# Moving the first loads to a second queue, and the fills and filler products around them, in a three-stage attention and MLP kernel

## The chip, the cores and the metric

The kernel runs on one NeuronCore of a Trainium2 chip. The metric is the time of one execution in microseconds on the device, given as the median of several runs. The core has five engines that run side by side, each through its own queue of instructions in a fixed order: PE (matrix products), DVE (vector), ACT (scalar and activation functions), POOL (general purpose) and SP, which only issues transfers between HBM and the on-chip memory. An instruction starts when it is at the head of its engine's queue and what it waits for has happened.

## What is computed

Linear attention mixed with causal attention, and behind it two MLPs with different activations. Cut to what matters:

```python
# q, k, v: (4, 8, 576, 64); M_prev: (4, 8, 64, 64); z_prev: (4, 8, 64); beta: (8,)
a     = softmax(causal(q @ k.T / 8));  local = a @ v
q_p   = elu(q) + 1
mem   = (q_p @ M_prev) / (q_p . z_prev + 1e-6)
g     = 1 / (1 + exp(-beta))
x     = g * mem + (1 - g) * local               # laid out as (2304, 512)
x     = softplus(x @ w_in) @ w_out              # 512 -> 2048 -> 512, weights given as float64
h     = x @ w2_in
P, Q  = a0 + a1 h + a2 h^2 + a3 h^3,  1 + |b0||h| + |b1|h^2
out   = (P / (Q + 1e-6)) @ w2_out
```

## The kernel before

All work is recorded first as operations with a key, and a planner (`Program.order`, L289) then lays every operation on its engine: it steps through an assumed timeline, takes on each engine the ready operation with the smallest key, and for operations that more than one engine can do (`flex`, L220) it also picks the engine. The result is a fixed order for each engine, which `emit` (L389) writes out; nearly all instructions therefore carry the line L392. A change at the start moves the assumed times behind it, and with them the order and the choice of engines of everything that follows, until the order falls into the same pattern again.

The attention runs in seven passes (`PASSES`, L63), each over one batch and some row tiles; a pass has two units of four heads (or four units of two). The first three passes work in float32: `attention32` (L1004) transposes q and k of a unit on PE (`transpose32`, L992, into banks of PSUM taken in turn from the list `B32`, L48), computes the scores of four heads on PE, masks them and takes their minimum on DVE (shown as CUSTOM_DVE_ANT_0), and exponentiates them on ACT. Between the passes run the blocks of the first MLP: `g1` (L1164) makes a pair of hidden tiles from the input weights, `g2` (L1207) multiplies them into the output. Before a float16 block, `xgroup` (L1084) splits its input x into a high and a low half per column chunk: four high halves on any of ACT, DVE and POOL (`scopy`, L533) and four low halves on DVE (one instruction) or POOL (two) (`low`, L553). `pmax` (L573) finds the scale that the split needs, by a reduction on POOL and a small product on PE.

The MLP weights come as float64, in pieces of 512 KB that SP loads as pairs of 32-bit words (`load_piece`, L1118) and DVE turns into float32 with three instructions a piece (`bits`, L1126: one TENSOR_SCALAR and two SCALAR_TENSOR_TENSOR on 128x512), or ACT and POOL share in it (`bits_abs`, L1132). There are 16 pieces of the input weights and 16 of the output weights, all in the first 100 us.

At the start, six raw buffers `RAW` (the landing places of q, k and v) have rows 64 to 127 filled with zeros by POOL (L1385), over all ten blocks of 64 columns; float32 units use only the first eight blocks, and fill them fully. `EARLY` (L29) says after which piece of the input weights the other first loads are issued: q and k of both first units after piece 0, v of unit 0 and the batch's M and z after piece 1, the three small constants (`beta` for the gate, and `a`, `b` of the second MLP) after piece 2. All are issued by SP. The gate's chain (`consts`, L603) is one Exp on ACT and six small instructions on DVE. PE is kept busy by 120 filler products of `mask` with itself (`WARM`, L1399), written into bank 0 and never read; the planner puts them wherever PE has nothing else.

Of the kernel before, what the change touches and what calls it, by code (L numbers as in the profile page):

```python
# [25 lines left out]

QLATE = 80
PORT = 0.8
EARLY = lambda load, u, consts, batch: (  # L29
    (lambda: load(u[0], 0, 1), lambda: load(u[1], 0, 1)),  # L30
    (lambda: load(u[0], 2), batch),
    (consts,),
    (lambda: load(u[1], 2),),
)
KEY_B0 = 30
KEY_S2 = 60
# [8 lines left out]
WR0 = 6  # L45
WARM = 120
FA32 = 3
B32 = (0, 1, 2, 3, 4, 5, 6)  # L48
PEC = 2.5
SIGN = ((0,), (0,))  # L50
SIGN2 = ((1,), (0, 0, 1))
# [5 lines left out]
SIGN3 = (0, 0, 1)  # L57
BACKLOG = 4000.0
NRAW = 6
NGH = 4  # L60
EXP = 0x7F800000

# [106 lines left out]
class Program:  # L169
# [14 lines left out]
    def add(self, eng, name, fn, kw, writes=()):  # L184
        rd, wr = [], list(writes)
        for k, v in kw.items():
            if is_ap(v):
                (wr if k in self.OUTS else rd).append(v)
        dma = 0
        if eng == "SP":  # L190
            o, i = kw["out"], kw["in_"]
            nb = width(o) * SIZE[o.dtype] * o.shape[0]
            if "transpose" in name:
                dur, dma = 1325, nb / 240.0

            else:
                run = min(SIZE[x.dtype] * (x.ap[-1][1] if x.ap[-1][0] == 1 else 1) for x in (o, i))
                dur, dma = 650 if o.shape[0] <= 64 else 475, nb / (360.0 if run >= 512 else 180.0)
        else:
            dur = cost(eng, name, kw)  # L200
        ported = shares_port(eng, name, kw)
        if self.cur is not None and self.cur.eng in (None, eng):
            op = self.cur
            op.eng = eng
            if eng in op.alts:
                op.alts[eng][0] += dur
                op.alts[eng][1].append((fn, kw))
            else:
                op.alts[eng] = [dur, [(fn, kw)]]
        else:  # L210
            op = self._new()
            op.eng = eng
            op.alts[eng] = [dur, [(fn, kw)]]
        op.dma = dma
        if ported:
            op.port.add(eng)
        self._deps(op, rd, wr)
        return op
# [70 lines left out]
    def order(self):  # L289
# [26 lines left out]
        while len(done) < len(self.ops):  # L316
# [52 lines left out]
            free[e] = end = s + dur  # L369
            for b in o.banks:  # L370
                held.setdefault(b, {})[e] = end
            if e == "SP":
                free["BULK"] = end
                dma_free = max(dma_free, s + min(dur, 650) + 625) + o.dma
                if dur > 1000:

                    free["SP"] = free["BULK"] = max(end, dma_free - 880)
                end = dma_free + 900
            done.append(o)
            for j in o.succ:  # L380
                q = self.ops[j]
                q.npred -= 1
                q.ready = max(q.ready, end + (max(LATENCY[e][x] for x in q.alts) if e in LATENCY else 0))
                if q.npred == 0:
                    release(q)
        self.span = max(free.values())
# [35 lines left out]
def attn_moe_moe2(ctx, tc, q, k, v, m_prev, z_prev, beta, w1i, w1o, w2i, w2o, ca, cb, out):  # L422
# [43 lines left out]
    def vw(o, shape, dtype):  # L466
        n = 1
        for s in shape:
            n *= s
        a = arena[:, o:o + n * SIZE[dtype] // 4]  # L470
        if dtype != F32:
            a = a.bitcast(dtype)
        if len(shape) == 1:
            return a
        names = [chr(97 + i) for i in range(len(shape))]
        return a.rearrange(f"p ({' '.join(names)}) -> p {' '.join(names)}", **dict(zip(names[1:], shape[1:])))
# [125 lines left out]

    def consts():  # L603
        P.bulk = True
        SP.dma_start(out=gg, in_=beta.partition_broadcast(128))
        SP.dma_start(out=aa, in_=ca.partition_broadcast(128))
        SP.dma_start(out=bb, in_=cb.partition_broadcast(128))
        P.bulk = False
        A.activation(out=gg, in_=gg, func=AF.Exp, scale=-1.0)
        ts(gg, gg, 1.0, None, ALU.add)  # L610
        V.reciprocal(gg, gg)
        ts(iog, gg, -1.0, 1.0, ALU.mult, ALU.add)
        ts(iog, iog, 2.0 ** -100, None, ALU.max)
        V.reciprocal(iog, iog)
        ts(iog15, iog, 2.0 ** -15, None, ALU.mult)
        A.activation(out=bb, in_=bb, func=AF.Abs)

    def consts2():
        A.activation(out=fa, in_=aa, func=AF.Abs)
# [79 lines left out]
        scopy(m.ms[:, :, 0, :], mr, m.s)  # L699
        stt(m.ms[:, :, 1, :], mr, m.s, m.ms[:, :, 0, :], ALU.mult, ALU.subtract)  # L700

    def load(u, *which):
        P.bulk = True
        load_(u, which)
        P.bulk = False

    def load_(u, which):
        p = u.p
        for i, (src, r, t0) in enumerate(((k, u.rk, 0), (q, u.rq, p.qts[0]), (v, u.rv, 0))):
            if which and i not in which:  # L710
                continue
            n = p.nk - t0
            r = r.rearrange("p (t h) d -> p h t d" if p.f32 else "p (h t) d -> p h t d", h=u.nh)
            if u.nh == 4:
                for t in range(n):
                    SP.dma_start(out=r[:, :, t, :], in_=src[p.b, u.h:u.h + 4, (t0 + t) * 128:(t0 + t + 1) * 128, :].rearrange("h p d -> p h d"))
            else:
                full = min(p.nk, 4) - t0
                for e in range(u.nh):
                    SP.dma_start(out=r[:, e, 0:full, :], in_=src[p.b, u.h + e, t0 * 128:(t0 + full) * 128, :].rearrange("(t p) d -> p t d", p=128))  # L720
                if p.nk == 5:
                    SP.dma_start(out=r[0:64, :, n - 1, :], in_=src[p.b, u.h:u.h + u.nh, 512:576, :].rearrange("h p d -> p h d"))
# [388 lines left out]
    def w_in_ap(w, pc):  # L1111
        p, i = divmod(pc, 2)
        return w.bitcast(U32)[i * 256:(i + 1) * 256, p * 512:(p + 1) * 512].rearrange("(c p) f -> p c f", p=128)

    def w_out_ap(w, pc):
        return w.bitcast(U32)[pc * 128:(pc + 1) * 128, :]

    def load_piece(ap, r):  # L1118
        P.bulk = True
        if len(ap.shape) == 3:  # L1120
            SP.dma_start(out=r.rearrange("p (c f) t -> p c (f t)", c=2), in_=ap)
        else:
            SP.dma_start(out=r.rearrange("p f t -> p (f t)"), in_=ap)
        P.bulk = False
# [194 lines left out]
    def w1_raw(which, pc):  # L1319
        if which == 0 and 0 <= pc - WR0 < 8:  # L1320

            return w1_o[pc - WR0].bitcast(U32).rearrange("p (f t) -> p f t", t=2)
        return vw(wraw[which][pc % len(wraw[which])], (512, 2), U32)

    def w1_load(which, pc):
        load_piece(w_in_ap(w1i, pc) if which == 0 else w_out_ap(w1o, pc), w1_raw(which, pc))

    def w1_place(which, pc, f32):
        if pc >= 16:
# [42 lines left out]
    def w2_early(i0, i1):  # L1372

        steps = [(0, pc) for pc in range(NST[0])] + [(1, pc) for pc in range(NST[1])]
        for i in range(i0, i1):
# [6 lines left out]
            w2_bits(which, pc, r, dst, a_t[1][:, 1024:1280].bitcast(BF16), vw(o, (512,), F32), SIGN3[i % len(SIGN3)])  # L1382
            SP.dma_start(out=w2d[which * 16 + pc], in_=dst)

    P.key = -180  # L1385
    for o in RAW:
        G.memset(vw(o, (10, D), F32)[64:128], 0.0)

    P.key = -150
    w1_load(0, 0)  # L1390
    P.add("POOL", "memset", lambda out: make_identity(nc, out), {"out": idf})
# [4 lines left out]

    P.pkey = 1e6
    for _ in range(WARM):
        PE.matmul(out=bank[0][:, 0:256], lhsT=mask[:, 0:128], rhs=mask[:, 0:256], start=True, stop=True)  # L1399
    early = EARLY(load, units, consts, lambda: batch_load(passes[0]))  # L1400
    for pc in range(16):
        P.key = -149 + pc
# [269 lines left out]
```

## Time and profile before

| | |
|---|---|
| median of three runs | 1015.4 us (1012.12, 1015.4, 1015.81) |
| the profiled execution, its own time | 1016.02 us |
| span of that execution's instructions | 1014.2 us |
| mean granted PE clock | 0.985 of full |
| busy share PE / DVE / ACT / POOL | 95% / 88% / 82% / 45% |

The span runs from the first instruction to the last; the execution's own time has 1.8 us around it. A busy PE is one with a product under way, filler products among them. Shares are means over stages with different limits, so the start, the middle and the end have to be read apart: a stage's limit is the engine that shows no idle time in it, while the others wait for it.

### The profile page before, as it was taken

The page shows a single profiled execution, that of the slowest core. Times are in us where ns is not written, and L with a number is a line of the kernel's source. Part 1 is how long each engine was busy: PE and PEld are TensorE (multiplying, and loading weights), DVE is VectorE, ACT ScalarE, POOL GpSimd, SP SyncE. Part 2 cuts the span into 40 slices and gives each one's busy share as a digit, 9 for nine tenths or more (in the row PEclk, how much of TensorE's full clock was granted, in tenths as well). Part 3 has the DMA queues.
Part 4 walks back from the last instruction along what each step waited for, and adds up shares of the span by engine and source line. Part 5 has one row for each costly group of instructions (what it writes and reads, how often), then busy time and mean ns, then how long its engine had stood idle before and what let it go on. Part 6 is the DMA issues. An engine that isn't in the chain of part 4 may idle for free. (4 is left out here: it accounts for less than half of the span.)

```text
span 1014.2 us, 22841 instructions
## 1 busy us (share of the span) xinstructions
PE 959.6 (95%) x8256; PEld 696.0 (69%) x8256; DVE 893.1 (88%) x2193; ACT 826.8 (82%) x1934; POOL 455.6 (45%) x516
## 2 busy tenths in 40 slices
PE   7779999999979999999899999899999999999998
PEld 6547688788769888888888998445555555555553
DVE  6999778988899988899878999988989889798886
ACT  4886988888869999899887888867888787887875
POOL 3121566873342243342325343655655455555443
PEclk9969999999989999999999999989999999999999
DMA  9997347568689979998998664000001000000000
GB/s 249 317 227 200 66 102 145 123 121 158 130 170 168 153 144 163 184 182 193 209 282 267 219 207 144 1 1 32 32 1 63 1 32 32 1 32 2 32 1 31
DMA packets 249889, 122.08 MB, mean 120 GB/s; under 512 B 219184, under 2 KB 225328, under 8 KB 249776
## 3 DMA queue, kind: packets, MB, share of 16 engines
q1 hardware_dynamic: 249776, 120.63, 51.4%
q8 instruction: 64, 1.05, 0.4%
q14 instruction: 49, 0.40, 0.1%
HBM read 65.54 MB, written 15.73 MB: 80 GB/s over the span
## 5 line engine op out<-in xcount | busy, mean ns | idle before, releaser
L392 PE MATMUL bank<-arena,w 128*128 128x160 f16 (+3 forms) x4288 | 414.8, 256 | 12.0 <-DVE arena L392 7.3
L392 PE MATMUL bank<-arena 128*128 128x384 f16 (+10 forms) x2852 | 355.6, 299 | 24.3 <-DVE arena L392 8.6
L392 PEld LDWEIGHTS <-w 128*128 128x128 f16 x3840 | 292.8, 98 | 29.9 <-issue 18.7
L392 ACT ACTIVATE arena<-bank,tiny 128x384 f32<-128x384 f32 (+8 forms) x504 | 276.3, 587 | 41.4 <-PE bank L392 34.6
L392 PEld LDWEIGHTS <-arena 128*128 128x128 f16 (+1 forms) x2464 | 165.8, 105 | 119.8 <-issue 29.8
L392 POOL TENSOR_TENSOR arena<-arena 128x384 f32<-128x384 f32 (+8 forms) x165 | 167.9, 1021 | 166.3 <-ACT arena L392 104.1
L392 PE MATMUL bank<-arena,gr 128*128 128x512 f16 x864 | 202.8, 380 | 1.2 <-POOL gr L392 1.1
L392 PEld LDWEIGHTS <-gr 128*128 128x128 f16 x864 | 84.5, 98 | 95.5 <-POOL gr L392 2.5
L392 POOL TENSOR_TENSOR gr<-arena,gr 128x384 f16<-128x384 f32 x96 | 90.6, 944 | 103.6 <-issue 81.2
L392 POOL TENSOR_SCALAR arena<-arena,tiny 128x512 f16<-128x512 f32 (+9 forms) x94 | 71.6, 768 | 102.2 <-DVE tiny L392 31.9
L392 ACT ACTIVATE bank<-bank,tiny 128x320 f32<-128x320 f32 (+5 forms) x192 | 103.3, 545 | 14.5 <-DVE tiny L392 9.5
L392 ACT ACTIVATE bank<-bank 128x320 f32<-128x320 f32 (+2 forms) x208 | 104.8, 504 | 1.6
L392 ACT ACTIVATE arena<-bank 128x320 f16<-128x320 f32 (+5 forms) x147 | 72.2, 501 | 29.6 <-PE bank L392 16.6
L392 PEld LDWEIGHTS bank<-arena,w 128*128 128x128 f32 x448 | 83.1, 190 | 12.4 <-issue 1.5
L392 DVE SCALAR_TENSOR_TENSOR arena<-arena,tiny 128x512 f16<-128x512 f32 (+5 forms) x101 | 89.8, 903 | 1.8 <-POOL arena L392 1.1
L392 DVE SCALAR_TENSOR_TENSOR bank<-bank,tiny,lt 128x384 f32<-128x384 f32 x96 | 59.6, 621 | 34.0 <-ACT lt L392 32.3
L392 ACT ACTIVATE lt<-arena,qe 128x384 f32<-128x384 f32 x96 | 59.0, 614 | 32.6 <-POOL arena L392 31.0
L392 DVE SCALAR_TENSOR_TENSOR arena<-arena,qe,lt 128x384 f32<-128x384 f32 x96 | 76.0, 791 | 0.7 <-ACT lt L392 0.7
L392 DVE SCALAR_TENSOR_TENSOR arena<-bank,tiny,arena 128x384 f16<-128x384 f32 (+4 forms) x112 | 64.0, 591 | 8.9 <-ACT arena L392 8.4
L392 DVE TENSOR_SCALAR tiny<-tiny 128x1 f32<-128x1 f32 (+8 forms) x349 | 64.5, 208 | 6.4 <-ACT bank L392 5.1
L392 DVE CUSTOM_DVE_ANT_0 bank<-bank,mask,tiny 128x384 f32<-128x384 f32 (+4 forms) x112 | 66.8, 605 | 2.4 <-PE bank L392 2.0
L392 PEld LDWEIGHTS bank<-arena 128*128 128x128 f32 (+3 forms) x412 | 43.2, 168 | 29.2 <-ACT arena L392 8.1
(122 smaller groups left out, 1143.3 us busy)
## 6 DMA issues: line engine op xcount, KB each, us to landing
arena<-in_moe_w_out_dram SPq DMA_DIRECT2D x32, 512.0 KB, 5.0
arena<-in_moe_w_in_dram SPq DMA_DIRECT2D x24, 512.0 KB, 5.1
w2d<-a SPq DMA_DIRECT2D x24, 256.0 KB, 3.0
arena<-w2d SPq DMA_DIRECT2D x24, 256.0 KB, 4.6
arena<-in_k_dram SPq DMA_DIRECT2D x44, 128.0 KB, 3.1
arena<-in_v_dram SPq DMA_DIRECT2D x44, 128.0 KB, 2.9
arena<-arena SPq DMA_DIRECT2D x32, 160.0 KB, 2.9
arena<-x2d SPq DMA_DIRECT2D x6, 768.0 KB, 4.3
```

The lines of the kernel that those rows point to most:

```text
L392: fn(**{k: (v.fn() if isinstance(v, Lazy) else v) for k, v in kw.items()})
```

## The change

- SP's queue starts with `beta`, then the k of both units, then v, M and z; the pieces of the input weights come behind them.
- ACT's queue issues the q of both units (four transfers) and the first `NACT` = 3 pieces of the input weights, between its table load and its first computations.
- The gate's chain (`gates`) is split from `consts` and is recorded at the very start; `a` and `b` are loaded after piece 8.
- The zero fills cover only the last two blocks of 64 columns of each raw buffer, which the first loads don't write.
- The filler products go into bank 3, and the list `B32` gives bank 3 up: the first pass's transposes and scores take six banks in turn instead of seven.
- The planner is told of transfers on ACT's queue.

```diff
 EARLY = lambda load, u, consts, batch: (
-    (lambda: load(u[0], 0, 1), lambda: load(u[1], 0, 1)),
-    (lambda: load(u[0], 2), batch),
-    (consts,),
+    (lambda: load(u[0], 2),),
+    (batch,),
     (lambda: load(u[1], 2),),
+    (), (), (), (), (), (consts,),
 )
-B32 = (0, 1, 2, 3, 4, 5, 6)
+B32 = (0, 1, 2, 4, 5, 6)
+NACT = 3
...
-        if eng == "SP":
+        if "dma" in name:
...
+            if o.dma and e != "SP":
+                dma_free = max(dma_free, end + 625) + o.dma
+                end = dma_free + 900
...
     def consts():
         P.bulk = True
-        SP.dma_start(out=gg, in_=beta.partition_broadcast(128))
         SP.dma_start(out=aa, in_=ca.partition_broadcast(128))
         SP.dma_start(out=bb, in_=cb.partition_broadcast(128))
         P.bulk = False
+        A.activation(out=bb, in_=bb, func=AF.Abs)
+
+    def gates():
+        SP.dma_start(out=gg, in_=beta.partition_broadcast(128))
         A.activation(out=gg, in_=gg, func=AF.Exp, scale=-1.0)
         ts(gg, gg, 1.0, None, ALU.add)
         V.reciprocal(gg, gg)
...
-    def load(u, *which):
-        P.bulk = True
-        load_(u, which)
+    def load(u, *which, eng=SP):
+        P.bulk = eng is SP
+        load_(u, which, eng)
...
     def w1_load(which, pc):
-        load_piece(w_in_ap(w1i, pc) if which == 0 else w_out_ap(w1o, pc), w1_raw(which, pc))
+        if which == 0 and pc < NACT:
+
+            A.dma_start(out=w1_raw(which, pc).rearrange("p (c f) t -> p c (f t)", c=2), in_=w_in_ap(w1i, pc))
+        else:
+            load_piece(w_in_ap(w1i, pc) if which == 0 else w_out_ap(w1o, pc), w1_raw(which, pc))
...
     P.key = -180
     for o in RAW:
-        G.memset(vw(o, (10, D), F32)[64:128], 0.0)
-
+        G.memset(vw(o, (10, D), F32)[64:128, 8:], 0.0)
+
+    P.key = -160
+    for u in units[0:2]:
+        load(u, 0)
+        load(u, 1, eng=A)
+        if u.i == 0:
+            gates()
...
     for _ in range(WARM):
-        PE.matmul(out=bank[0][:, 0:256], lhsT=mask[:, 0:128], rhs=mask[:, 0:256], start=True, stop=True)
+        PE.matmul(out=bank[3][:, 0:256], lhsT=mask[:, 0:128], rhs=mask[:, 0:256], start=True, stop=True)
```

What the planner makes of it is seen at three places. The first is the start of DVE's queue. In the names, `w_2_80` is the tile that takes the first two weight pieces, `gg` and `iog` belong to the gate, ISA with `mask` is a masked score, and `arena` holds everything else. Before, behind three small instructions:

```order
L392 TENSOR_SCALAR w_2_80<-arena 128x512
L392 SCALAR_TENSOR_TENSOR w_2_80<-arena,w_2_80 128x512
L392 TENSOR_SCALAR w_2_80<-arena 128x512
L392 SCALAR_TENSOR_TENSOR w_2_80<-arena,w_2_80 128x512
L392 COPY mask_101<-mask 64x64 x2
L392 SCALAR_TENSOR_TENSOR w_2_80<-arena,w_2_80 128x512 x2
L392 SCALAR_TENSOR_TENSOR arena<-arena 128x512
L392 ISA a_98,tiny<-bank_71,mask 128x256
```

And now, at the same place:

```order
L397 TENSOR_SCALAR gg<-gg 128x8
L412 RECIPROCAL gg<-gg 128x8
L397 COPY mask_101<-mask 64x64
L397 TENSOR_SCALAR iog<-gg 128x8
L397 COPY mask_101<-mask 64x64
L397 TENSOR_SCALAR iog<-iog 128x8
L412 RECIPROCAL iog<-iog 128x8
L397 TENSOR_SCALAR iog_104<-iog 128x8
L397 COPY arena<-bank_69 128x512
L397 SCALAR_TENSOR_TENSOR arena<-arena 128x512
L397 ISA a_98,tiny<-bank_72,mask 128x256
```

The two weight pieces have gone from ahead of the first masked score to behind the eight masked scores of unit 0; the gate's chain and a copy out of PSUM stand there in their place.

The second is the start of ACT's queue, where `gg` is the gate, `wacc` takes a sum over a weight piece, `arena<-arena 128x512` are the Relu and Exp on a unit's q, and `arena<-bank` a copy of a transpose. Before:

```order
L1245 ACT_TABLE_LOAD
L392 ACTIVATE a_99,wacc<-w_2_80 128x512
L392 ACTIVATE arena<-bank_70 128x512
L392 ACTIVATE arena<-arena 128x512
L392 ACTIVATE a_99,wacc<-w_2_80 128x512
L392 ACTIVATE arena<-bank_69 128x512
```

And now:

```order
L1252 ACT_TABLE_LOAD
L397 DMA arena<-in_q_dram 128x4x64 x4
L397 ACTIVATE gg<-gg 128x8
L397 DMA arena<-in_moe_w_in_dram 128x2x512 x3
L397 ACTIVATE arena<-arena 128x512 x2
L397 ACTIVATE arena<-bank_70 128x512
```

Seven issues, with the gate's Exp between them, now stand ahead of ACT's first work on the attention; the copy of the other transpose (`bank_69`) has gone to DVE, as the first fence shows, and the sums over the weight pieces behind unit 0. On PE, 18 filler products stand ahead of the first transpose (there were 6), then 2 and 8 to the first score (there were 10 and 12), so 28 in all as before, with q's transposes now ahead of k's.

The third is POOL's queue at the split of pass 3's x (128x576 a chunk), some 130 instructions into its program. TENSOR_SCALAR on 128x576 makes a high half or the first step of a low half, TENSOR_TENSOR the second step of a low half; TENSOR_REDUCE belongs to `pmax`, and what follows is attention. Before:

```order
L392 TENSOR_REDUCE tiny<-tiny 1x1
L392 TENSOR_SCALAR arena<-arena,tiny 128x576 x3
L392 TENSOR_TENSOR arena<-arena 128x576
L392 TENSOR_SCALAR arena<-arena,tiny 128x10x64
L392 TENSOR_TENSOR arena<-arena,tiny 128x384
```

And now:

```order
L397 TENSOR_REDUCE tiny<-tiny 1x1
L397 TENSOR_SCALAR arena<-arena,tiny 128x576 x3
L397 TENSOR_TENSOR arena<-arena 128x576
L397 TENSOR_SCALAR arena<-arena,tiny 128x576
L397 TENSOR_TENSOR arena<-arena 128x576
L397 TENSOR_TENSOR arena<-arena,tiny 128x384
```

POOL makes two low halves of this split now, where it made one; DVE makes two high and two low halves (it made one and three), and ACT none (it made one high half). On PE, 36 products of 128x256 and two scores stand between the small product of `pmax` and the first product on the split x, where there were 24 and two scores.

From the last quarter of the program on, the second MLP, the order on PE, DVE, ACT and POOL is the same in both programs.

## Rows read from the trace of the kernel before

**Rows 1.** The page's part 1: busy time, share of the span, instructions.
```profile
PE 959.6 (95%) x8256; PEld 696.0 (69%) x8256; DVE 893.1 (88%) x2193; ACT 826.8 (82%) x1934; POOL 455.6 (45%) x516
```

**Rows 2.** Busy time by stretches: stretch, length, engines (instructions), granted clock, DMA share, GB/s.
```profile
0.00:20.00 20.00, 14.41 (x103) 11.52 (x104) 10.51 (x38) 9.85 (x30) 5.70 (x17) 1.00 0.95 214
20.00:40.00 20.00, 15.21 (x127) 11.00 (x125) 20.00 (x61) 14.19 (x45) 5.27 (x6) 1.00 1.07 354
...
80.00:100.00 20.00, 19.80 (x117) 15.14 (x115) 20.00 (x62) 11.77 (x37) 2.12 (x4) 1.00 0.69 190
100.00:120.00 20.00, 17.28 (x112) 11.78 (x113) 14.49 (x59) 19.48 (x56) 10.28 (x15) 1.00 0.13 30
```

**Rows 3.** DVE in order of time: start, length (us), instruction, [idle before, releaser].
```profile
4.88 0.75 DVE L392 TENSOR_SCALAR w<-arena 128x512 uint32<-128x512 uint32 x1 [3.80 <-DMA arena<-in_moe_w_in_dram]
...
7.26 0.36 DVE L392 COPY mask<-mask 64x64 bf16<-64x64 bf16 x2
...
12.60 0.69 DVE L392 SCALAR_TENSOR_TENSOR arena<-arena 128x512 f32<-128x512 f32 x1 [3.53 <-ACT arena L392]
...
14.07 0.42 DVE L392 CUSTOM_DVE_ANT_0 a<-bank,mask 128x256 f32<-128x256 f32 x1 [0.78 <-PE bank L392]
...
16.30 0.69 DVE L392 COPY arena<-bank 128x512 f32<-128x512 f32 x1
...
19.31 0.17 DVE L392 TENSOR_SCALAR gg<-gg 128x8 f32<-128x8 f32 x1
```

**Rows 4.** POOL at the start, in order of time.
```profile
0.72 3.48 POOL L405 MEMSET arena<- 64x640 f32 x6 [0.29 <-POOLq L1656]
...
4.26 0.21 POOL masks.py:197 MEMSET arena<- 128x128 f32 x1
```

**Rows 5.** PE at the start, in order of time.
```profile
5.26 1.46 PE L392 MATMUL bank<-mask 128*128 128x256 bf16 x6 [5.26 <-POOL mask L405]
...
8.22 2.34 PE L392 MATMUL bank<-mask 128*128 128x256 bf16 x10
10.35 1.06 PE L392 MATMUL bank<-arena 128*128 128x128 f32 x4
...
12.90 2.17 PE L392 MATMUL bank<-arena 64*128 64x256 f32 x20
14.91 7.70 PE L392 MATMUL bank<-mask 128*128 128x256 bf16 x69
```

**Rows 6.** SP's and ACT's queues at the start, and SP's waits in 0 to 20 us.
```profile
0.73 1.28 ACT L1245 ACT_TABLE_LOAD   x1 [0.73 <-PEq L1656]
...
1.75 1.01 SPq L392 DMA_DIRECT2D arena<-in_k_dram  x2
...
SPq L392 <- POOL arena L405: 2.3, 3, 1.8
```

**Rows 7.** The split of pass 3's x, in order of time, PE, POOL and DVE.
```profile
279.18 2.87 PE L392 MATMUL bank<-arena,w 128*128 128x256 f16 x25
...
279.86 2.98 POOL L392 TENSOR_SCALAR arena<-arena,tiny 128x576 f16<-128x576 f32 x3 [1.57 <-DVE tiny L392]
...
282.92 1.65 POOL L392 TENSOR_TENSOR arena<-arena 128x576 f16<-128x576 f32 x1
284.63 5.45 PE L392 MATMUL bank<-arena,w 128*128 128x192 f16 x44 [1.94 <-POOL arena L392]
...
293.77 1.15 PE L392 MATMUL bank<-arena,w 128*128 128x192 f16 x12 [3.19 <-DVE arena L392]
```

**Rows 8.** The same split: one group of instructions by shape, and one stretch.
```profile
L392 POOL TENSOR_SCALAR arena<-arena,tiny 128x576 f32<-128x576 f32 x1 | 1.2, 1238 | 0.0
...
285.00:286.00 1.00, 1.00 (x9) 0.91 (x8) 0.98 (x8) 0.00 (x0) 0.00 (x0) 0.50 0.53 182
```

**Rows 9.** PE's groups by line, 115 to 640 us: busy, mean ns, idle before, releasers.
```profile
L392 PE MATMUL bank<-arena,w 128*128 128x160 f16 (+3 forms) x4176 | 388.6, 253 | 12.0 <-DVE arena L392 7.3 <-POOL arena L392 1.9 <-DVE tiny L392 1.3
L392 PE MATMUL bank<-arena 128*64 128x64 f16 (+9 forms) x1444 | 116.2, 263 | 9.7 <-DMA arena<-arena 5.9 <-DVE arena L392 2.5 <-DVE tiny L392 0.9
```

More of the change, by code (lines that the diff above doesn't have):

```diff
@@ L382, in order @@
                 q.npred -= 1
-                q.ready = max(q.ready, end + (max(LATENCY[e][x] for x in q.alts) if e in LATENCY else 0))
+                q.ready = max(q.ready, end + (max(LATENCY[e][x] for x in q.alts) if e in LATENCY and not o.dma else 0))
                 if q.npred == 0:
@@ L615, in consts @@
         ts(iog15, iog, 2.0 ** -15, None, ALU.mult)
-        A.activation(out=bb, in_=bb, func=AF.Abs)
     def consts2():
@@ L700, in batch_scale, with load_ @@
         stt(m.ms[:, :, 1, :], mr, m.s, m.ms[:, :, 0, :], ALU.mult, ALU.subtract)
-    def load(u, *which):
-        P.bulk = True
-        load_(u, which)
+    def load(u, *which, eng=SP):
+        P.bulk = eng is SP
+        load_(u, which, eng)
         P.bulk = False
-    def load_(u, which):
+    def load_(u, which, eng):
         p = u.p
@@ L715, in load_ @@
                 for t in range(n):
-                    SP.dma_start(out=r[:, :, t, :], in_=src[p.b, u.h:u.h + 4, (t0 + t) * 128:(t0 + t + 1) * 128, :].rearrange("h p d -> p h d"))
+                    eng.dma_start(out=r[:, :, t, :], in_=src[p.b, u.h:u.h + 4, (t0 + t) * 128:(t0 + t + 1) * 128, :].rearrange("h p d -> p h d"))
             else:
```

## The prediction

> **What bounds the kernel now.** I read the page's busy shares first: PE is busy 95% of the span [rows 1], filler products included, so the whole looks bound by PE. The stretches say where it is not [rows 2]. From 120 us on PE has few gaps; before that it is another engine. In 0 to 20 us DVE is busy 10.51 us, so it is idle for 9.5; in 20 to 40 and again in 80 to 100 it is busy 20.00 of 20, that is, without a gap; in 100 to 120 it has gaps again (14.49), ACT is full (19.48) and PE busy 17.28. So the first hundred microseconds are paced by the sum of DVE's work: three instructions for each of 32 weight pieces, and the masked scores of the first four units. What stands ahead of DVE's unbroken stretch counts in full; what is earlier on another engine counts only if DVE gets work from it.
>
> DVE in order of time tells what its 9.5 idle microseconds are [rows 3]: 3.80 until the first weight piece lands, 3.53 until unit 0's q is through ACT, 0.78 until the first scores, the rest small. Between 4.88 and 9.07 (12.60 less 3.53) it turns two weight pieces, so that work lies in time that would otherwise be lost. The first masked score starts at 14.07.
>
> Behind that, from 115 to 640 us, PE's groups show 12.0 and 9.7 us of idle time ahead of the products on weights and on attention [rows 9], released by DVE, POOL and DMA. These gaps come from the order, and the order is rebuilt. From 640 us on both programs have the same order, so I carry that part over unchanged.
>
> **The change part by part.**
>
> The *zero fills* shrink from 640 to 128 columns. Six took 3.48 us [rows 4]; a fill of 128 columns of 128 rows took 0.21, so six cost at most some 1.2. All that POOL makes behind them, identity and mask, comes 2.2 us earlier, and the fillers start at about 3.0 instead of 5.26 [rows 5]. SP's waits for these fills, 2.3 us in three places [rows 6], vanish.
>
> The *loads*: k had to wait for the issue of two weight pieces, and started at 1.75; now it starts at about 1.2, behind `beta`. The pair of k took 1.01 to issue, so I take 0.5 an issue. No row shows an issue by ACT; I price it like SP's, between 0.35 and 0.9 (SP's issues spread that far where they queue). The table load ends at 2.01 [rows 6]; four issues of q end at about 4.0, three pieces at about 5.7, at worst 8.5. ACT's next work on the attention's path is a copy behind the transposes, which by the next step but one end at 8.0 and 9.4, so these issues are hidden; without that cover they would cost what they last, 3.5 to 6.3.
>
> The first 20 us moved data at a DMA share of 0.95, 20 to 40 at 1.07 [rows 2]. The transfers are the same bytes as before. The Trainium skill says so of this very step (DMA: Bandwidth & Descriptors, Issuing engines are not separate DMA queues): transfers started by different engines run on the same 16 DMA engines and interleave, and a second issuer saves only the time of issuing. The trace agrees that there is little room, with those shares. By that rule q and k still land together, and the change is worth at most two issues ahead of k.
>
> The *first scores*: 18 fillers stand ahead of the transposes. The ten from 8.22 on took 2.34 us, or 0.213 each between starts; the 69 from 14.91 on took 7.70, or 0.111 [rows 5]: PE was at 1.2 GHz first and at 2.4 later. At the slow price 18 take 3.8 and end at 6.9; q and k, 1 MB at 214 GB/s, have landed by then (2.0 + 4.7). Four transposes took 1.06; two sets and two fillers end at about 9.4, ACT's copy and eight fillers at 10.2 to 11.0. The scores start there instead of at 12.90, **1.9 to 2.7 us earlier**, and the first masked score at 11.4 to 12.2.
>
> But on *DVE*, the pace of this part, the two weight pieces have moved from ahead of that point to behind it. What stands ahead now: 0.25 of small instructions, six of the gate's at 0.17 [rows 3], the mask's copies (0.36 [rows 3]), one copy out of PSUM and one SCALAR_TENSOR_TENSOR, 0.69 each: 3.0 us. DVE is thus idle for 8.4 to 9.2 us, against 9.5. The lead of the attention shrinks to **0.3 to 1.1 us of DVE time**, and one more copy of a transpose falls to DVE (0.69 [rows 3]). The gate's chain is only moved, at no cost. I take 0.4 gained, from 0.4 lost to 1.1 gained.
>
> *Bank 3* for the fillers and six banks in turn: the fillers write a bank that nobody waits for; unit 0 uses six, so the ring wraps only at unit 1, whose transposes wait for copies that are done. Nothing, and at most one wait like the 0.78 in [rows 3]. *`a` and `b` late*: they are read after 100 us; nothing.
>
> The *rebuilt order* I can price at one place. At the split of pass 3's x, POOL worked 2.98 + 1.65 us from 279.86, and PE, which had run out of products at 282.1, started at 284.63 with POOL's end [rows 7]. Now a second low half stands behind: 1.24 [rows 8] and 1.65, so POOL ends 2.9 later. PE has 12 more products ahead of that wait, at 2.87/25 each: 1.4 us of cover. **1.5 lost**, between 0 (DVE and PE late themselves) and 2.9 (no cover).
>
> The sum, against the profiled execution's 1016.0 us: 1016.0 - 0.4 + 1.5 = 1017.1. That execution was 0.6 above the median of 1015.4, so a median of **1016.5**.
>
> **The rivals.**
>
> *The rebuilt order loses PE's gaps.* If the two waits at 284.63 and 293.77 (1.94 + 3.19) were covered, PE would also not fall to the granted 0.50 behind the first [rows 7, 8]: 44 products took 5.45 there, and would take 4.2 at the 0.096 each (1.15/12) of those at 293.77, so 1.2 was lost. That is 6.3 us: 1016.5 - 1.5 - 6.3 = **1008.7**. As much again may come out of the other 16.6 us of gaps [rows 9]; half of it gives 1005.5. For it: the gaps are many, and each hangs on which engine the planner picked. Against: at the one place I can follow, it goes the other way.
>
> *The split's wait grows into a slow stretch.* POOL's second low half ends 7.6 us after its first instruction; if PE runs out of products as early as before, it idles over 5 us there, 2.9 more. If it then stays at half speed through all 56 products up to the next work, they take 10.8 instead of 5.4 at 0.096 each; 1.2 of that was paid before, so 4.2 are new: 1016.5 - 1.5 + 2.9 + 4.2 = **1022.1**. It decides from the point where PE ends the previous block more than 2 us ahead of POOL's second TENSOR_TENSOR. For it: POOL's row in the order. Against: the 12 more products.
>
> *The lead counts in full.* If not DVE's sum but the attention's chain paces the first 100 us, all of the 2.3 us stay: 1016.5 - 1.9 = **1014.6**. DVE's 20.00 of 20 speaks against it.
>
> *It doesn't do what it says.* If the pieces on ACT's queue land late, because they share the DMA engines with k, v, M and z, DVE waits for them. It asks for both first pieces at about 15; 2 MB at 214 GB/s have passed by 11.5, and 2.5 MB by 14. A delay of 2 us would give **1018.5**.
>
> **How the numbers follow.** I give my forecast with its two near rivals (1014.6, 1018.5) 52%: these lie within 0.5% of 1015.4, that is 1010.3 to 1020.5, about what a measurement of this kernel can tell from no change. PE's gaps going: 27%, faster. The split's wait and gaps like it: 21%, slower. The forecast's own range is 1012 to 1020; the range to hold 8 in 10 reaches into both other cases, to 1007 and to 1023.
>
> **What would show it.** Right: the first masked score between 11 and 12.5 us, DVE busy without gaps soon after, and full again from 20 to 100; PE waiting 3 to 4 us for POOL at the split of pass 3's x; the stretch from 640 us on as long as before. Wrong: DVE's unbroken stretch ending 2 us or more earlier, with PE's continuous work starting as much earlier; DVE waits for weight pieces; or PE's idle sum between 115 and 640 us, 22 in the two groups, off by more than 5.

## The result and the profile after

The changed kernel takes 1018.13 us (median of 9 runs, 1017.23 to 1021.6); beside it the kernel before takes 1013.18 (9 runs, 1012.08 to 1015.81). The ratio is 1.0051, with a 95% interval of 1.0038 to 1.0064: **5 us slower**. The profiled execution took 1017.94 us, with a span of 1016.2. The one of the kernel before (1016.02, span 1014.2) was 2.8 us above the median of its nine, so the two traces differ by 2.0 us where the medians differ by 5.

The start did what was forecast. These are DVE, ACT's queue and PE of the changed kernel in order of time (start, length, instruction, [idle before, releaser]); they answer to [rows 3, 5, 6]:

```profile
0.76 3.58 ACTq L397 DMA_DIRECT2D arena<-in_q_dram  x4
...
2.70 3.75 PE L397 MATMUL bank<-mask 128*128 128x256 bf16 x18 [2.70 <-POOL mask L410]
...
6.29 0.60 PE L397 MATMUL bank<-arena 128*128 128x128 f32 x4
6.39 2.14 ACTq L397 DMA_DIRECT2D arena<-in_moe_w_in_dram  x3
...
6.93 0.69 DVE L397 COPY arena<-bank 128x512 f32<-128x512 f32 x1 [0.84 <-PE bank L397]
...
7.38 1.04 PE L397 MATMUL bank<-mask 128*128 128x256 bf16 x8
...
8.64 1.29 ACT L397 ACTIVATE arena<-arena 128x512 f32<-128x512 f32 x2 [4.05 <-DMA arena<-in_v_dram]
...
10.47 2.17 PE L397 MATMUL bank<-arena 64*128 64x256 f32 x20 [2.05 <-ACT arena L397]
...
11.63 0.42 DVE L397 CUSTOM_DVE_ANT_0 a<-bank,mask 128x256 f32<-128x256 f32 x1 [0.98 <-PE bank L397]
```

The releaser named at 8.64 cannot be v: its first transfer lands at 9.25. What ACT stood behind are its own issues, as e8 below tells. The first masked score starts at 11.63, where it started at 14.07. But the stretches of the changed kernel show how little of that is DVE's (columns as in [rows 2]):

```profile
0.00:20.00 20.00, 15.25 (x127) 12.69 (x128) 11.30 (x46) 11.17 (x32) 5.09 (x19) 1.00 1.01 250
20.00:40.00 20.00, 18.99 (x146) 14.15 (x144) 20.00 (x56) 15.50 (x51) 2.27 (x4) 1.00 1.08 339
40.00:60.00 20.00, 9.60 (x44) 7.01 (x42) 19.97 (x52) 15.31 (x45) 13.12 (x4) 0.68 0.86 209
```

DVE is busy for 11.30 us of the first 20 (10.51 before), so it is 0.8 ahead; ahead of the first masked score its idle time is 8.70 instead of 9.05, which is 0.35. PE, which gets its scores and fillers done early, stands still for half of 40 to 60.

What was not forecast is behind: PE's groups from 115 to 640 us, in the changed kernel (columns as in [rows 9]):

```profile
L397 PE MATMUL bank<-arena,w 128*128 128x160 f16 (+3 forms) x4168 | 390.2, 254 | 9.4 <-DVE arena L397 6.9 <-POOL arena L397 2.5
L397 PE MATMUL bank<-arena 128*64 128x64 f16 (+9 forms) x1430 | 112.3, 259 | 13.1 <-DMA arena<-arena 8.0 <-DVE arena L397 3.5 <-DVE tiny L397 0.7
L397 PE MATMUL bank<-tiny,one 1*128 1x5 f32 (+1 forms) x56 | 10.1, 255 | 5.1 <-POOL tiny L397 5.0 <-ACT arena L397 0.2
L397 PE MATMUL bank<-a,arena 128*64 128x256 f16 (+1 forms) x24 | 1.4, 247 | 1.2 <-DMA a<-arena 1.2
```

The two groups of [rows 9] have 22.5 us of idle time ahead of them, where they had 21.7. With the two small groups it is 28.8, where it was 24.5: before, the group on `a` and `arena` had none, and the other this:

```profile
L392 PE MATMUL bank<-tiny,one 1*128 1x5 f32 (+1 forms) x54 | 10.3, 257 | 2.8 <-POOL tiny L392 2.1 <-ACT arena L392 0.6
```

For all that follows I read two things from each trace, stretch by stretch: PE's idle time, and what PE loses at the granted 0.50, 1.2 instead of 2.4 GHz (half the time spent there). The second is the number behind the +. "Old" and "new" say whose order of the instructions a kernel has in the stretch; the kernels are those of the next section.

| PE's idle us + slow loss | 115 to 300 | 300 to 540 | 540 to 640 | 640 to 700 |
|---|---|---|---|---|
| before (old) | 7.4 + 3.4 | 13.2 + 0 | 3.9 + 0 | 4.3 + 3.4 |
| e1 (old) | 8.4 + 1.7 | 11.5 + 0 | 4.8 + 0 | 4.3 + 1.7 |
| e6 (new to some 310, then old) | 8.9 + 0 | 14.2 + 0 | 5.0 + 1.7 | 4.3 + 3.4 |
| changed (new) | 6.3 + 3.4 | 16.6 + 1.7 | 6.0 + 1.7 | 4.2 + 0 |
| e2 (new) | 6.9 + 5.1 | 13.6 + 0 | 7.2 + 3.4 | 4.2 + 0 |
| e10 (new, one product held back) | 6.7 + 3.4 | 14.6 + 1.7 | 8.5 + 5.1 | 4.3 + 0 |

From 115 to 640 the changed kernel loses 35.7 us against 27.9, that is 7.8 more: 1.0 less before 300, 8.8 more behind. From 640 to 700 it gets 3.5 back.

The stretches are cut at fixed times and not at the same work, so these sums are rough. A second measure is the **lag**: for the n-th instruction of one form and tiles on an engine, its start in the one trace less its start in the other, as a median. By the lag the changed kernel is 0.2 us ahead at 115 us, some 6.4 behind at 640 and 2.0 behind from 700 on. Both measures compare one pair of traces, which differ by 2.0 us; the 5 us are the difference of the medians.

### The profile page after: what moved, and what is told of

Read it like the earlier page. It is cut to its first block, busy times and chain, and to the rows that moved or that the text cites. A ratio compares the mean times of both kernels' runs of the same rounds, so it can differ in the third digit from the quotient of the medians.

```text
span 1016.2 us, 22852 instructions
## 1 busy us (share of the span) xinstructions
PE 959.5 (94%) x8256; PEld 700.3 (69%) x8256; DVE 889.8 (88%) x2199; ACT 823.5 (81%) x1925; POOL 462.9 (46%) x520
## 4 chain that ended last, share of the span: by engine, by line
PE 47%; DVE 23%; ACT 11%; DMA 9%; issue 4%; SPq 3%; POOL 1%; POOLq 0%; DVEq 0%; ACTq 0%
PE bank L397 47%; DVE arena L397 9%; ACT arena L397 5%; DVE bank L397 4%; ACT bank L397 4%; DVE w L397 4%; DVE tiny L397 3%; DMA arena<-arena 3%; SPq L397 3%; DMA arena<-in_moe_w_in_dram 2%; DVE a L397 2%; DMA arena<-in_v_dram 1%; ACT a L397 1%; DVE gr L397 1%; POOL arena L397 1%
## 5 line engine op out<-in xcount | busy, mean ns | idle before, releaser
L397 PE MATMUL bank<-arena 128*128 128x384 f16 (+8 forms) x2852 | 353.6, 297 | 30.7 <-ACT arena L397 9.5
L397 ACT ACTIVATE arena<-bank,tiny 128x384 f32<-128x384 f32 (+7 forms) x505 | 276.4, 585 | 47.1 <-PE bank L397 39.9
L397 POOL TENSOR_TENSOR arena<-arena 128x384 f32<-128x384 f32 (+7 forms) x163 | 168.3, 1035 | 163.7 <-ACT arena L397 113.3
L397 ACT ACTIVATE bank<-bank,tiny 128x384 f32<-128x384 f32 (+5 forms) x192 | 102.8, 543 | 14.0 <-DVE tiny L397 9.4
L397 POOL TENSOR_SCALAR arena<-arena,tiny 128x640 f16<-128x640 f32 (+9 forms) x95 | 71.1, 756 | 88.5 <-DVE tiny L397 34.1
L397 ACT ACTIVATE arena<-bank 128x320 f16<-128x320 f32 (+5 forms) x147 | 71.6, 497 | 27.9 <-PE bank L397 13.5
L397 DVE SCALAR_TENSOR_TENSOR arena<-arena,tiny 128x384 f16<-128x384 f32 (+5 forms) x100 | 84.0, 853 | 0.4 <-POOL arena L397 0.3
L397 DVE SCALAR_TENSOR_TENSOR arena<-arena,qe,lt 128x384 f32<-128x384 f32 x96 | 68.9, 717 | 0.1
```

The source lines that it names most:

```text
L397: fn(**{k: (v.fn() if isinstance(v, Lazy) else v) for k, v in kw.items()})
```

## The experiments

Two theories stood at first. **A**: the start is worth nothing either way, and the order that the planner rebuilt behind it costs the 5 us. **B**: the start itself costs them (ACT's queue, late landings, a bank less). C, in the expectations, is that the two have to meet.

**One half of each kernel: e1, e2, e5, e6, e7, e9.** Both kernels have the same 5611 units of work for the planner, so the order of one can be put behind the start of the other. The planner's own order holds up to a seam, a time of its plan; what is left follows in the other kernel's order and on its engines, from a table:

```diff
     def emit(self):
-        for o in self.order():
+        late = late_order()
+        n = {i for i, _ in late}
+        plan = [o for o in self.order() if o.idx not in n]
+        for i, e in late:
+            self.ops[i].eng = e
+            plan.append(self.ops[i])
+        for o in plan:
             for fn, kw in o.alts[o.eng][1]:
```

> The changed kernel's own instructions for what the planner starts in the first 60 us of its plan; everything behind that in the order and on the engines that the kernel before has. Theory A (the start is worth nearly nothing, the rebuilt order behind it costs the 5 us): ratio to the kernel before 0.998 to 1.001, that is -2 to +1 us; on the trace the gaps of PE and the slow stretches between 115 and 640 us are those of before (24.6 us in the three groups, two slow stretches). Theory B (the start itself costs it: issues on ScalarE, late landings, one bank less): ratio 1.004 to 1.006, with a lag already there at 100 us. Theory C (neither alone, they have to meet): 1.002 to 1.004.

Measured: 1.0015 (0.9999 to 1.0032), between A and C. The trace is plainer than the time. By the lag, PE's first scores come 2.4 us earlier than in the kernel before, and most of what it does from 25 to 50 us some 8 us earlier; at 110 us the difference is 0.0 on each of PE, DVE, ACT and POOL, and it stays within 0.2 us up to 260. So **the start buys nothing**: the 2.4 us of lead are gone by 60 us. Nor does it cost anything there: in all eight traces that have the new start (the changed kernel, e1, e5 to e8, e10, e12) PE's lag at 110 to 120 us lies between -0.3 and 0.3.

> The other half: the start of the kernel before (the first 60 us of its plan), everything behind it in the order and on the engines of the changed kernel. Theory A: ratio 1.003 to 1.006 (+3 to +6 us), with PE's gaps between 115 and 640 us up by 4 or more against the kernel before and four slow stretches where that has two. Theory B: ratio 0.998 to 1.001. Theory C: 1.002 to 1.003.

Measured: 1.0029 (1.0010 to 1.0047), just below A and within C. The trace is the changed kernel's once more: at 640 us its instructions are 6.0 us later than those of the kernel before; in the changed kernel they are 6.4 later. Against C speaks that no trace with the new start lags at 110 us. As times alone, e1's 1.5 us and e2's 2.9 would nearly add up to the 5; e1's trace can't rule that out by its length, since its execution (1012.27) is 3.7 below its median.

> As e1_new_start_old_rest, with the seam later: the changed kernel's order for the first 110 us of its plan, that of the kernel before behind. Theory A (start worth nothing, the rest costs): ratio 0.999 to 1.002, and on the trace a lag behind the kernel before of 0.0 to 0.5 us at 120 us that stays so until 640. Theory B (the start costs 1.5 us or more, as the median of e1 may mean): ratio 1.001 to 1.003 and a lag of 1 us or more that is there by 120 us.

Measured: 1.0017 (1.0003 to 1.0031). The time allows both. On the trace the lag is -1.4 us from 120 to 400, so there is no cost by 120 us; the profiled execution loses it behind 400, where it has the old order.

> The seam at 300 us of the plan: the changed kernel's order up to there, that of the kernel before behind. It holds the split of pass 3's x with its second low half on POOL. Theory D (the loss is gathered in many places between 115 and 640 us, half of it behind this seam): ratio 1.000 to 1.003. Theory E (the split of pass 3 is where it is lost): ratio 1.004 to 1.006, all of it. Gaps of PE before 300 us on the trace: about 25.6 as in the changed kernel, without the 4.0 that follow there up to 340.

Measured: **0.9997** (0.9980 to 1.0014). E falls: the new start and the new order up to 300, the split of pass 3 among it, cost nothing together. As the changed kernel as a whole has 1.0051, the loss is behind that seam. The other half, which should confirm it, is e9, and that one can't be read, as told next. e6 has the same start as e1 and e5, so their +1.5 us is not a price of the start, which the lags at 110 us exclude too; where it comes from behind 110 us stays open.

> The seam at 480 us of the plan. Theory D: more than with the seam at 300, 1.002 to 1.004, short of the whole 1.005. Theory E: the same as with the seam at 300. A third reading, F (the loss comes in the last part only, 480 to 640 us, where the first of the two MLPs ends): within 0.001 of the kernel before.

> The complement of e6_new_until_300: the order of the kernel before up to 300 us of the plan, that of the changed kernel behind. Theory G (the loss lies behind 300 us): ratio 1.003 to 1.007, with the 2 us wait of PE for the one-column product and a slow stretch behind it near 545 us. Theory H (it lies before 300, or is only there when both halves come together): 0.999 to 1.002.

Measured: 1.0081 (1.0065 to 1.0097) for e7, and 1.0116 (1.0085 to 1.0147) for e9. Both are worse than either whole kernel, and neither settles anything: each has one wait at its seam that neither kernel has. Whom PE waits for (us in total, times, longest), first of e7 in 510 to 520 us, then of e9 in 310 to 325:

```profile
PE bank L420 <- DVE arena L420: 4.4, 1, 4.4
```

```profile
PE bank L417 <- DMA arena<-arena: 3.9, 1, 3.9
```

Two plans cut together where much is in flight make a new gap; only the seams in calm places (60, 110 and 300 from new to old) can be read.

**Another order by other means: e3, e4.** One line each in the kernel before:

```diff
-PEC = 2.5
+PEC = 2.6
```
```diff
-BACKLOG = 4000.0
+BACKLOG = 3900.0
```

> The kernel before with one number of its planner moved, PEC from 2.5 to 2.6 ns for a product. No instruction is added or removed; the plan is the same up to about 200 us and behind it 79 instructions are on another engine. Theory A (any rebuilding of the order moves the time by some us, whatever caused it): ratio off 1 by 0.002 to 0.007, either sign. Theory B (the rebuilt order is worth nothing, so an order as good as the old one gives the old time): within 0.001 of 1.

> The kernel before with another number of its planner moved, BACKLOG from 4000 to 3900 ns. No instruction is added or removed; the plan is the same up to about 79 us, and behind 115 us 126 instructions are on another engine (124 by the change itself). Theory A: ratio off 1 by 0.002 to 0.007, either sign; the size of the change's own +0.005 is then what a rebuilt order does by itself. Theory B: within 0.001 of 1.

Measured: 1.0066 (1.0050 to 1.0082) and 1.0166 (1.0148 to 1.0183). Neither adds or drops any work, and they cost 6.7 and 17 us. So a rebuilt order (the choice of engines with it) costs as much as the change, or three times as much. With the change that makes three rebuilt orders and three losses: the old order is better than each of these, and more were not drawn. In e4 the largest piece is at the start of the second MLP, where the lag against the kernel before goes from 6.4 to 14.3 us (waits of PE for whom: us in total, times, longest, 640 to 700 us):

```profile
PE bank L392 <- DVE arena L392: 8.3, 5, 4.9
PE bank L392 <- POOL tiny L392: 3.0, 1, 3.0
```

**The second issuer: e8.** The start of the changed kernel with one issuer, old order behind:

```diff
-NACT = 3
+NACT = 0
...
-        load(u, 1, eng=A)
+        load(u, 1)
```

> The changed kernel's start with the queries and the first three weight pieces issued by SP again; order behind 60 us of the plan as in the kernel before. By DVE's pace (what lands a little later at the start is made up, since DVE has weight pieces to do): first masked score at 11.6 to 13 us, and at 110 us no lag against e1, within 0.5 us. If the second issuer is what matters: first masked score at 13 us or later, and a lag of 1 us or more at 110 us.

Measured in a single run: 1014.26 us. The first masked score comes at 11.22, **0.4 us earlier** than with two issuers and earlier than expected, and at 110 us the lag is 0.0. ACT in order of time shows the difference:

```profile
3.42 0.21 ACT L424 ACTIVATE gg<-gg 128x8 f32<-128x8 f32 x1 [1.42 <-DMA gg<-in_beta_dram]
6.76 0.60 ACT L424 ACTIVATE arena<-bank 128x512 f32<-128x512 f32 x1 [3.13 <-PE bank L424]
```

Here ACT copies the first transposes at 6.76. In the changed kernel its next instruction on q stands behind the three issues of weight pieces (6.39 to 8.53) and starts at 8.64, though the first unit's q has landed by 5.73 and its transposes end at 6.89. Each of those issues waits for the semaphore of an earlier transfer, which they take over: by the trace they were released at 6.37, 7.54 and 8.14, as three of the k transfers landed, and took 0.37 to 0.40 themselves. With one issuer the planner also puts k's transposes ahead of q's, so the 0.4 us are not the issuer's alone.

**The place: e10.** In the last of the stretches, 540 to 640, the kernels of the table with the new order lose 7.7 to 13.6 us, those with the old one 3.9 to 6.7 (e9, which has the new order there but comes 10 us later, 6.1). Here PE of the changed kernel:

```profile
543.92 0.38 PE L397 MATMUL bank<-tiny,one 1*128 1x1 f32 x2 [0.89 <-POOL tiny L397]
544.23 1.00 PE L397 MATMUL bank<-arena,w 128*128 128x160 f16 x12
547.30 0.38 PE L397 MATMUL bank<-tiny,one 1*128 1x1 f32 x2 [2.07 <-POOL tiny L397]
```

The second one-column product hands round the largest value of the second MLP's first input, whose first products run at 625.70 us. e10 holds it back, with what depends on it:

```diff
+HOLD = 18000.0
...
+        plan = self.order()
+        late = {self.held.idx}
+        for o in plan:
+            if o.idx in late:
+                late |= o.succ
+        until = self.held.start + HOLD
+        plan.sort(key=lambda o: max(o.start, until) if o.idx in late else o.start)
+        for o in plan:
```

> The changed kernel with one product of PE, and what depends on it, held back by 18 us of the plan: the one-column product that hands the largest value of the second MLP's first input to all partitions. In the changed kernel PE stands 2.07 us before it at 545.23, and the clock falls to half for 3.41 us behind it, though the value is first needed near 622 us. Theory I (that place is a large part of the loss): the wait and the slow stretch are gone, -2.1 to -3.8 us, ratio to the kernel before 1.0013 to 1.003. Theory J (what comes next is late anyway, so that other waits take its place): no change, 1.004 to 1.006.

Measured: 1.0076 (1.0059 to 1.0093). J holds and more: another wait took its place. PE and DVE of e10:

```profile
542.20 1.00 PE L405 MATMUL bank<-arena,w 128*128 128x160 f16 x12
546.19 6.03 PE L405 MATMUL bank<-arena,w 128*128 128x160 f16 x51 [2.99 <-DVE arena L405]
```

```profile
541.58 0.55 DVE L405 SCALAR_TENSOR_TENSOR bank<-bank,tiny,arena 128x320 f32<-128x320 f32 x1
543.98 1.75 DVE L405 TENSOR_REDUCE tiny<-arena 128x1 f32<-128x1536 f32 x1 [1.85 <-DMA arena<-x2d]
545.65 0.48 DVE L405 TENSOR_TENSOR arena<-bank,arena 128x320 f16<-128x320 f32 x1
```

And DVE of the changed kernel, then of the kernel before, at the same place:

```profile
545.11 1.75 DVE L397 TENSOR_REDUCE tiny<-arena 128x1 f32<-128x1536 f32 x1 [0.94 <-DMA arena<-x2d]
546.78 0.48 DVE L397 TENSOR_TENSOR arena<-bank,arena 128x320 f16<-128x320 f32 x1
...
547.97 0.22 DVE L397 TENSOR_SCALAR tiny<-bank 128x1 f32<-128x1 f32 x2
```

```profile
547.74 0.16 DVE L392 TENSOR_SCALAR tiny<-bank 128x1 f32<-128x1 f32 x1
...
548.62 1.75 DVE L392 TENSOR_REDUCE tiny<-arena 128x1 f32<-128x1536 f32 x1
550.29 0.48 DVE L392 TENSOR_TENSOR arena<-bank,arena 128x320 f16<-128x320 f32 x1
```

PE's products start as this TENSOR_TENSOR ends (546.13 and 546.19 in e10; 547.26 and 547.61 in the changed kernel, with the one-column product at 547.30 between). Ahead of it on DVE stands the reduction of the second MLP's first input, and that waits for a transfer: 1.85 us in e10, 0.94 in the changed kernel, none in the kernel before, where the scale of the last pass's x (the TENSOR_SCALAR on tiny<-bank) also goes first, 0.03 us behind its product; in the changed kernel that scale is read 3.7 us after its product. So the product that I held back was a bystander, and DVE's order is what is left as the cause of this place. That is argued from these rows: a kernel with the reduction itself held back was not tried.

**A better version: e11, e12.** In the traces with the old order PE waits twice for DVE just behind 640 us, and runs slowly after it. These are PE of the kernel before and the two stretches around it:

```profile
654.19 2.11 PE L392 MATMUL bank<-arena 128*128 128x384 f16 x12 [0.78 <-DVE arena L392]
656.13 2.11 PE L392 MATMUL bank<-arena,gr 128*128 128x512 f16 x9
661.44 4.00 PE L392 MATMUL bank<-arena 128*128 128x384 f16 x12 [3.20 <-DVE arena L392]
```

```profile
640.00:660.00 20.00, 17.46 (x92) 8.90 (x91) 20.00 (x31) 15.75 (x30) 13.28 (x14) 1.00 0.01 2
660.00:680.00 20.00, 18.56 (x86) 9.14 (x86) 17.31 (x27) 12.27 (x25) 10.21 (x10) 0.83 0.00 1
```

DVE is busy 20.00 of 20, with splits of output weights among it that are wanted one by one, a block of some 3.9 us each. e11 is the kernel before with these due later; e12 adds the same line to e10:

```diff
-            P.key = KE + (pc * 10 - 60 if which else pc - 150)
+            P.key = KE + (pc * 10 + 10 if which else pc - 150)
```

> The kernel before with the splits of the second MLP's output weights due 7 blocks later in the planner's keys (KE + 10 pc + 10 for KE + 10 pc - 60); the plan is the same up to 610 us. In the kernel before PE waits 0.78 and 3.20 us for DVE at 653 and 658 us, where DVE makes these splits in a row, and runs at half speed for 6.8 us behind it. If DVE's splits are what it waits for: both waits go, -4 to -7 us, ratio 0.993 to 0.996. If the second MLP's own chain of DVE is the bound there: within 0.001 of 1.

Measured: **0.9942** (0.9925 to 0.9960), 1007.91 us (median of 11 runs, 1003.59 to 1012.56): faster than both kernels, by 5.9 us against the one before. The same two stretches:

```profile
640.00:660.00 20.00, 20.00 (x109) 10.54 (x108) 19.23 (x34) 16.26 (x34) 12.36 (x12) 1.00 0.01 2
660.00:680.00 20.00, 20.00 (x109) 10.48 (x108) 20.00 (x32) 16.80 (x34) 12.46 (x12) 1.00 0.00 1
```

PE has no gap left there, and the clock stays at 1.00. On the trace the lag against the kernel before goes from +0.6 at 640 us to -6.5 at 665, 7.1 us at one place.

> The changed kernel with both: the product held back as in e10_hold_back, the splits due later as in e11_old_later_splits. If the two are apart from each other, the sum of theirs: ratio 0.995 to 0.999, that is 4 to 9 us faster than the changed kernel. If only one of them holds, what that one gives.

Measured: 1.0031 (1.0011 to 1.0051). That is 4.5 us below e10, so the later splits work with the new order too. Against the changed kernel itself it is 2 us, since the hold, which was to give 2 to 4, cost 2.5 in e10; the sum that was expected is missed by that.

## Why the prediction held, and where it didn't

The forecast was 1016.5 and the range 1007 to 1023; the time, 1018.13, lies in it. As a difference the forecast was poorer: +1.1 us against +5 measured. That the absolute number came so near is luck: its base, the median of three runs (1015.4), was 2.2 above the median of nine.

- **What bounds the start**: right. DVE sets the pace; e1 shows that an attention earlier by 2.4 us is worth 0.0 at 110 us. The rival by which the lead counts in full falls. The sign "full again from 20 to 100" held to 60 us only: from 60 to 100 DVE idles 2.1 us, where it idled 1.0.
- **Fillers and first scores**: right in sum (11.63, forecast 11.4 to 12.2), by other parts. The fillers start at 2.70 (forecast 3.0). The transposes took 0.60 for four, not 1.06, as PE was at the faster of the two paces of [rows 5] from about 6.3 on: 18 fillers took 3.75 before, 0.21 each, and 8 took 1.04 behind, 0.13 each. (The column of the granted clock reads 1.00 for both.) ACT then took back what that won: PE waits 2.05 for it ahead of the scores.
- **DVE's lead**: forecast 0.3 to 1.1, less 0.69 for a copy. I set 8.4 to 9.2 against 9.5, which is the idle time of all 20 us; ahead of the first masked score it was 9.05. Measured 0.35 less there, 0.8 in the 20 us, and one more COPY of 128x512; in e1 nothing is left at 110 us. I took 0.4 gained; it is 0.0.
- **ACT's issues are hidden**: wrong, though at no cost. I had them at 2.0 to 5.7 us, at worst 8.5, behind transposes that end at 8.0 and 9.4; they end at 8.53, and the transposes at 6.89 and 7.55. The first issues ran beside the table load, but I had left out that an issue can wait for a landing, with ACT's work on q behind it in the same stream. By the Trainium skill (DMA: Bandwidth & Descriptors, Issuing engines are not separate DMA queues) a second issuer saves only the time of issuing; e8 agrees, and here even that was not won: one issuer has its first score at 11.22, two at 11.63. As DVE paces this part, neither counts. The rival of late pieces did not come: the first two landed at 11.63 and 14.50 us, and DVE took them up at 15.13 without a gap.
- **The split of pass 3**: this term was mis-sized. I had 1.5 lost for the second low half on POOL, with a wait of 3 to 4 us. PE's two waits there are these:

```profile
285.83 1.52 PE L397 MATMUL bank<-arena,w 128*128 128x192 f16 x9 [1.97 <-POOL arena L397]
287.91 2.99 PE L397 MATMUL bank<-arena,w 128*128 128x192 f16 x26 [0.56 <-POOL arena L397]
```

PE splits its block and waits 1.97 for the first low half, as long as in [rows 7], and only 0.56 for the second, since nine products cover it: 0.6 more than the 1.94 there, not 1.5. (PE had run out of products at 282.69 there, 284.63 less 1.94, and not at 282.1, as I read it.) The 3.19 us wait behind [rows 7] is gone as well. So of the rival of the lost gaps one wait of two came true at this place; up to 340 us 4.0 of idle time came in its stead, where the kernel before had none. e6, which has the split and the waits up to some 310 us, shows no cost. The rival of the slow stretch did not come: one slow stretch, with a loss of 1.7 us, where the kernel before had two.
- **The step that failed** is "the rebuilt order I can price at one place". I carried the other gaps at zero, and looked for trouble only in the two groups of [rows 9]; these two grew by 0.8 us, so that my sign for their sum (off by more than 5) stayed silent. The small groups grew by 3.5 (2.8 to 6.3), the loss in slow stretches by 3.4 (3.4 to 6.8), and most of it lies behind 300 us. The trace could not tell me its size; e3 and e4 could have, since an edit of one number of the planner shows the spread of rebuilt orders: +6.7 and +17 us. With these two known, slower was the likelier side.
- **From 640 us on "unchanged"**: wrong, and so is its ground. The order is the same from the last quarter on: DVE's instructions follow the same order in both traces from 750 us, ACT's from 749. At 640 it is not yet; here is the reduction of the second MLP's third input on DVE, before and in the changed kernel:

```profile
625.50 1.75 DVE L392 TENSOR_REDUCE tiny<-arena 128x1 f32<-128x1536 f32 x1
```

```profile
675.02 1.74 DVE L397 TENSOR_REDUCE tiny<-arena 128x1 f32<-128x1536 f32 x1
```

PE's idle time from 640 to 700 is nearly the same (4.3 and 4.2 us), but it lies in seven short waits, the longest 1.2, instead of three, the longest 3.2, and the clock stays up: 3.5 us come back, 4.4 by the lag. It is the place at which e11 gains, and the splits of the output weights stand in another order there too. So the rebuilt order seems to win here a part of what e11 wins; that is read from the rows and was not tried by itself.

## What to carry to other kernels

Where a planner sets the order, an edit at one end rebuilds the order of everything behind it, and here three rebuilt orders of three were worse than the tuned one: hold the order behind the edit fixed to weigh the edit, and move one number of the planner to see what any rebuilt order costs. An earlier start counts only on the engine that paces the stretch. And when an engine waits for something it doesn't yet need, look one engine further before moving it: the wait may only be the first of two that end at the same moment.

## What was not expected of the hardware

- **An issue on ACT's queue can hold ACT.** Four issues of q span 3.58 us and three of pieces 2.14; 0.37 to 0.53 us of each is the issue, the rest is waiting for earlier landings. ACT has nothing between 4.59 and 8.64 but these. The first two and the start of the third (0.76 to 2.32) ran beside the table load (0.72 to 2.00).
- **POOL beside an unbroken run of DVE.** The same product of M with the gate took 10.46 us in the changed kernel, and 1.61 in the kernel before:

```profile
39.85 10.46 POOL L397 TENSOR_TENSOR arena<-arena,gg 128x512 f32<-128x512 f32 x1 [10.26 <-DMA arena<-in_M_prev_dram]
```

```profile
40.98 1.61 POOL L392 TENSOR_TENSOR arena<-arena,gg 128x512 f32<-128x512 f32 x1 [2.30 <-DMA arena<-in_M_prev_dram]
```

DVE did integer instructions on weight pieces all the while. In the changed kernel they kept their 0.41 and 0.67 us, 18 in a row, until one of 0.67 took 1.52 from 49.34, and POOL ended at 50.31; in the kernel before the one at 41.61 took 1.53, and POOL ended at 42.59. The Trainium skill (Trainium Architecture — The Big Picture, What this means for kernel authors) says that these two engines share a port pair by an exclusive lock; the rows agree that one of them stands still. Spans on POOL are rough, and nobody waited for this one.
- **What a slow stretch costs.** Behind waits of 1.2 to 3.6 us the granted clock fell to 0.50, for PE a loss of 1.7 to 3.4 us each time; but seven short waits with a sum of 4.2 us, behind 640 in the changed kernel, brought none. Whether one comes varies between runs of one order: from 115 us on the kernel before lost 1.7, 1.7 and 3.4 us so, and e1, which has its order there, 1.7 and 1.7; e1's profiled execution took 1012.27 us.
